# A four-layer attention kernel on one core: four hundred operations of the last quarter take other places in the order table

## The chip, the core and the metric

The kernel runs on one core of a Trainium2 chip. Its engines run beside each other, each in the order of its own instruction stream: TensorE (PE in the profile; PEld is its loading of weights), VectorE (DVE), ScalarE (ACT) and GpSimd (POOL). SyncE (SP) and ACT issue the transfers here. The metric is the device time of one execution in microseconds (us).

## The reference

Four residual layers in the order A, B, A, B act on x of 2048 rows and 512 columns, with 32 heads of 16:

```python
def _A_ref(x, wqkv, wo):                      # attention within a window of 256 rows
    ...
    scores = jnp.einsum("bhqd,bhkd->bhqk", q, k) * (Dh ** -0.5)
    mask = (idx[:, None] - idx[None, :] >= 0) & (idx[:, None] - idx[None, :] < W)
    scores = jnp.where(mask[None, None], scores, -1e9)
    p = _softmax(scores, axis=-1)
    o = jnp.einsum("bhqk,bhkd->bhqd", p, v)
    return (...)(o, 0, 2, 1, 3).reshape(B, S, D) @ wo
def _B_ref(x, wqkv, wo):                      # linear attention
    ...
    phi = lambda t: jnp.where(t > 0, t + 1, jnp.exp(t)) + 1e-6
    pq, pk = phi(q), phi(k)
    kv = jnp.einsum("bhsd,bhse->bhde", pk, v)
    num = jnp.einsum("bhqd,bhde->bhqe", pq, kv)
    den = jnp.einsum("bhqd,bhd->bhq", pq, z)[..., None] + 1e-6
    return (...)(num / den, 0, 2, 1, 3).reshape(B, S, D) @ wo
x = x + _A_ref(_layernorm(x), A_wqkv, A_wo)   # and so on: B, A, B
```

## The kernel before

The residual stays on chip as 16 tiles of 128 rows (`xres`), in four superblocks I of four tiles. The program is a list of 2583 operations, and each says which engines it may run on, what it depends on and which buffers it takes: one of 8 PSUM banks of `psb`, or a place in a small ring (`xn`, `oT`, `xnT`, `pks`, `vs`, `ln`). No scheduler decides the order when the kernel is built. The string `ORDER` (line 214 on) holds it, written out by hand or by a search: an entry such as `2537P1` says that operation 2537 comes next, on PE, with PSUM bank 1; A is ACT, V DVE, G POOL, S SP; `4F2` is four filler matmuls into bank 2 (L463). `Planner.run` walks the string and emits every operation on its engine. So the places in the string set the order of each engine, and an engine waits at an instruction whose input or buffer is not ready, with all that stands behind it. A bank that was given to one operation is free for the next only when its last reader is done.

The steps that the change and the prediction touch, with their lines:

- **Attention of the second A layer** (the last of it lies at 305 to 371 us of the trace): scores on PE (L823), two exps of 128x1024 on ACT (L834, L837), masks on DVE (L852, a multiply for one or two windows of 64) or POOL (L857, an affine select for each window), product with v on PE (L880), division on DVE (L893, L894). Projections are four matmuls in two halves (L537), and a copy out of PSUM is L527 on ACT or DVE.
- **Closing layernorm**: the attention's output projection is added to the residual (DVE L736, L738), then the squares on ACT (L612), the inverse root on ACT (L592, L593) or POOL (L595, L596), the normalized tile on ACT (L626), DVE or POOL (L628), and its transpose by PE (L566), copied out by ACT or DVE (L569).
- **phi of layer B**: exp on ACT (L948), min and add on DVE or POOL (L951), add and max on DVE (L954); v's copy is L981; kv is summed by PE (L995) and DVE (L1002).
- **End stage**: kv times wo (L1063, woB to `wkv`). For each pair of superblocks PE makes the denominators (L1078), ACT its logarithm and exp, which is the reciprocal (L1083, L1084), and a bf16 part of it (L1090), DVE the rest (L1093); PE spreads that to all rows (L1106) and DVE multiplies `pqT` by it, two columns at a time (L1110). Then each tile is projected by `wkv` (L537) and added to the residual: on DVE (L729, or in two halves L704 for tile 2), or, for tiles with i%3 = 1, by an ACT copy (L720) and a POOL add (L724). A put (L731, L707) to the output is issued by SP or ACT.

The tile order of the last projections is 1, 3, 2, 0, 7, then 4, 5, 6 (with the second pair's spreads between), then those of I=3 and at the end those of I=2. An ACT copy, a POOL add or a put is behind each.

Of the kernel before, what the change touches and what calls it, by code (L numbers as in the profile page):

```python
# [214 lines left out]
24S 2G 5G 4G 15H 14H 53V0 0G 11G 58V1 17H 54A 68A1 6G 16H 63V2 3G 59G 55V20 18H 19H 1G 10F0 56P5 60V0 64G 61P1 57A 62V  # L215
9G 69V 2F2 74P0 75A 7V 1F2 70P1 65V0 72P6 71A 66P3 20H 92P7 73A 21H 67V 93P 120P42 94A 80P0 122A 95S 76P6 81V 88P1 121A
77V 89P 23H 22H 78P2 350V0 90A 123G 124P64 82P0 126A 79V 351G 91S 84P1 125A 340V1 133P24 83A 127G 96P6 85V 134A 106P0
10G 97V 104P1 135A 107V 137P26 341G 105V 139A 86P0 138A 146P46 87V 27S 116P1 147A 335V2 98P0 117P 148A 99V 336G 150P42
136V 25S 112P0 345V3 151A 149G 113P 152A 159P64 118A 337V31 140G 102P2 114V 161A 35S 128P1 346G 129P 103V 130P 131P 160A
342V1 163P42 153G 132V 26H 165A 115S 347V2 162G 3F0 188P06 164A 634V1 100P2 189A 166G 141P5 154P4 101V 155P 142P 36H  # L220
143P 190A 635G 144P 28H 352V0 193P02 145V 156P 119S 12G 157P 194A 108P6 158V 167P7 168P 191G 169P 195A 109V 170P 199P04
171V 348P6 200A 353P3 196G 349V 338P7 172S0 354V 343P6 201A 339V 204P02 638V0 379P7 29S 205A 380P 202G 344V 636V32 192G
206A 381V 2F5 210P04 361P6 639G 637S 642V1 362P 211A 208G 110P7 363V 212A 31S 203G 224P02 30H 198G 640V0 225A 383P5 213G
111V 384P 197V 382S 226A 643G 229P06 385V 214P4 215P 230A 646V0 216P 32H 358P5 644V3 231A 647G 217P 228V 235P02 641S
218V 359P 209G 236A 207G 355P7 360V 219P6 645S 237A 933V2 240P04 356P 241A 648V1 220P 239G 357V 221P 649S 232G 222P 233G
242A 246P02 227V 387P7 234G 386S 247A 223V 388P 238G 245V 389V 248A 395P04 13G 664P6 396A 665P 249V 934G 390S 250P7 667V
251P 397A 244G 400P02 666V 252P 243G 401A 941V0 253P 399G 391P6 392P 254V 402A 176S1 405P04 393V 364P7 406A 403G 365P
255P6 407A 366V 394S 410P02 256P 398V 257P 411A 404V 409G 258P 678P7 259V 412A 679P 416P04 680V 260S3 417A 657P3 414G
408V 415G 658P 276V 418A 650P2 264S2 660V 432P06 651P 413V 434A 419G 420V 51S 367P5 421V 368P 433A 659V 422P4 423P 369V
424P 653A 33S 436G 437P06 425P 438A 652V 427P5 428P 426V 429P 439A 430P 442P02 431V 376P4 443A 440G 377P 942G 34H 370P5  # L230
444A 378V 447P06 371P 441V 935V20 448A 682P4 372V 683P 449A 435V 453P02 684V 675P5 454A 676P 446V 451G 685S 452V 450V
455A 2F4 469P60 677V 445V 471A 457V 2F4 474P24 458V 456V 49S 937V1 475A 464P1 459P0 465P 476A 460P 466P 41S 461P 470A
467P 462P 479P24 463V 173P7 472G 480A 39S 468V 174P 481A 175V 484P02 654P6 945V2 936S 655P 485A 482G 373P7 473V 477G
656V 374P 938G 486A 681S 490P04 375V 690P6 483G 491A 691P 946G 487V 492A 177P7 489V 939V0 178P 488G 478V 506P02 692A
494V 495G 493V 507A 693S 943V1 2F4 496P5 179V 501P4 508A 497P 511P06 498P 512A 510V 509G 502P 180V1 499P 47S 503P 513A
500V 504P 181G 516P02 686P5 517A 514V 505V 940S 184V3 518A 3F7 521P06 671P4 45S 48H 687P 522A 519V 947V2 672P 688V 523A
527P20 674V 948S 265P5 266P 529A 524V 526G 661P7 673V 944S 515G 662P 528A 267V 525G 261P6 520V 694P40 663A 689S 531V
532G 262P 695A 530V 533P7 263V 534P 696A 535P 272V0 699P42 538P6 700A 539P 698G 540P 182G01 536P 701A 541P 537V 704P04
# [1210 lines left out]
```

## Time and profile before

| | us |
|---|---|
| time, median of 3 runs | 416.8 |
| lowest and highest run | 416.27, 418.25 |
| span of the profiled execution | 414.3 |
| TensorE busy in it | 395.2 (95%) |
| ACT, DVE, POOL busy | 368.8 (89%), 355.0 (86%), 239.2 (58%) |

The span is the time from the first to the last instruction that the profiler recorded of one execution; about 2.5 us of the median lie outside it. In all but the last of the page's 40 slices the granted clock of TensorE is 9 tenths or more. The chain of waits that ended last is for 66% on PE, 15% on ACT and 12% on DVE. The rows on which the prediction rests are in the section after next.

### The profile page before, as it was taken

How to read it: one execution, taken by the hardware profiler on the slowest of the kernel's cores; microseconds unless marked ns; L12 is line 12 of the kernel's file. 1: busy time of each engine (PE TensorE's matmuls, PEld its weight loads, DVE VectorE, ACT ScalarE, POOL GpSimd, SP SyncE). 2: the span in 40 equal slices, each digit the busy share in tenths (PEclk: the TensorE clock that was granted, in tenths of full speed). 3: DMA queues.
4: the chain of work that ended last, by engine and by line, in shares of the span. 5: the costliest groups of instructions: out<-in, count | busy, mean ns of one | idle time of the engine just before them, and what ended most of it. 6: DMA issues, size and time to landing. Idle time of an engine off the chain costs nothing.

```text
span 414.3 us, 15373 instructions
## 1 busy us (share of the span) xinstructions
PE 395.2 (95%) x6277; PEld 219.3 (53%) x6347; DVE 355.0 (86%) x844; ACT 368.8 (89%) x496; POOL 239.2 (58%) x505
## 2 busy tenths in 40 slices
PE   7998999999999999999999999999999999999995
PEld 3565555555555555643565555555555555565342
DVE  5899898888769988689998999998789588889895
ACT  5999999999999999678999999999999999977731
POOL 7578524344576667923774688554427476585432
PEclk9999999999999999999999999999999999999998
DMA  8233226440313122100032212322111311300024
GB/s 245 83 95 100 64 76 110 110 77 24 89 25 80 35 55 26 28 4 0 22 72 41 55 45 64 71 38 53 41 49 34 54 30 40 54 14 14 3 69 138
DMA packets 65306, 24.11 MB, mean 58 GB/s; under 512 B 46160, under 2 KB 65232, under 8 KB 65232
## 3 DMA queue, kind: packets, MB, share of 16 engines
q1 hardware_dynamic: 63168, 21.65, 23.5%
q10 hardware_dynamic: 2064, 1.44, 1.1%
q8 instruction: 50, 0.82, 0.8%
q14 instruction: 24, 0.20, 0.2%
HBM read 6.29 MB, written 2.10 MB: 20 GB/s over the span
## 4 chain that ended last, share of the span: by engine, by line
PE 66%; ACT 15%; DVE 12%; issue 4%; POOL 2%; ACTq 0%; POOLq 0%; DVEq 0%
PE psb L537 41%; PE psb L880 14%; PE psb L823 8%; ACT pt L834 7%; ACT pt L837 7%; DVE pt L852 2%; DVE kall L788 1%; PE psb L995 1%; DVE qT L527 1%; PE psb L566 1%; DVE kall L773 1%; PE psb L463 1%; DVE vst L527 1%; PE psb L1106 1%; DVE ln L661 1%
## 5 line engine op out<-in xcount | busy, mean ns | idle before, releaser
L857 POOL TENSOR_SCALAR_AFFINE_SELECT pt<-pt 128x256 bf16<-128x256 bf16 x285 | 121.3, 453 | 110.2 <-ACT pt L837 66.7
L837 ACT ACTIVATE pt<-psb 128x1024 bf16<-128x1024 f32 (+2 forms) x156 | 156.2, 1017 | 4.4 <-PE psb L823 3.0
L834 ACT ACTIVATE pt<-psb 128x1024 bf16<-128x1024 f32 (+2 forms) x156 | 156.7, 1014 | 3.6 <-PE psb L823 2.3
L880 PEld LDWEIGHTS <-pt 128*128 128x128 bf16 x2880 | 81.4, 96 | 16.5 <-issue 5.0
L880 PE MATMUL psb<-vbd,pt 128*128 128x34 bf16 x2880 | 85.1, 178 | 2.4 <-ACT pt L834 1.0
L537 PE MATMUL psb<-xnT,wA 128*128 128x512 bf16 (+1 forms) x305 | 65.1, 335 | 2.2 <-DVE o_sb L894 0.3
L537 PE MATMUL psb<-wB,xnT 128*128 128x512 bf16 x237 | 62.4, 379 | 1.7 <-issue 0.5
L823 PE MATMUL psb<-qT,kall 32*128 32x256 bf16 (+4 forms) x1664 | 62.6, 242 | 0.6 <-ACT pt L834 0.4
L537 PEld LDWEIGHTS <-xnT 128*128 128x128 bf16 x384 | 33.4, 97 | 37.0 <-issue 5.3
L823 PEld LDWEIGHTS <-kall 32*128 32x128 bf16 x1664 | 28.0, 92 | 45.8 <-issue 42.2
L852 DVE TENSOR_TENSOR pt<-pt,tri 128x512 bf16<-128x512 bf16 (+1 forms) x133 | 49.5, 399 | 2.8 <-ACT pt L837 1.9
L537 PEld LDWEIGHTS <-wA 128*128 128x128 bf16 x320 | 27.4, 97 | 26.1 <-issue 7.7
L537 PE MATMUL psb<-woA,oT 128*128 128x512 bf16 x120 | 32.8, 380 | 1.2 <-issue 0.6
L537 PE MATMUL psb<-wA,xnT 128*128 128x512 bf16 x115 | 32.3, 380 | 1.5 <-ACT pt L837 0.5
L537 PE MATMUL psb<-xnT,wB 128*128 128x512 bf16 x119 | 32.1, 380 | 0.9 <-issue 0.5
L537 PE MATMUL psb<-wkv,pqT 128*128 128x512 bf16 (+1 forms) x126 | 30.2, 373 | 0.5 <-issue 0.2
L894 DVE TENSOR_TENSOR o_sb<-psb,rall 128x256 bf16<-128x256 f32 x64 | 27.2, 424 | 2.4 <-DVE rall L893 0.2
L893 DVE RECIPROCAL rall<-psb 128x16 f32<-128x16 f32 x64 | 16.1, 251 | 13.7 <-PE psb L880 9.4
L661 DVE BATCH_NORM_STATS2 ln<-xres 128x6 f32<-128x512 f32 (+1 forms) x39 | 26.6, 682 | 1.2 <-DMA xres<-in_A_x_dram 1.1
L596 POOL TENSOR_TENSOR ln<-ln,mhalf 128x1 f32<-128x1 f32 x38 | 22.0, 578 | 3.2
L948 ACT ACTIVATE pks<-psb 128x512 bf16<-128x512 f32 x32 | 19.5, 614 | 3.8 <-PE psb L537 3.4
L527 DVE CAST qT<-psb 128x512 bf16<-128x512 f32 (+1 forms) x32 | 19.2, 602 | 3.9 <-PE psb L537 3.7
(133 smaller groups left out, 523.6 us busy)
## 6 DMA issues: line engine op xcount, KB each, us to landing
vbd<-vst SPq DMA_DIRECT2D x128, 34.0 KB, 1.9
wB<-in_B_wqkv_dram SPq DMA_DIRECT2D x6, 256.0 KB, 3.5
out_dram<-ost SPq DMA_DIRECT2D x10, 128.0 KB, 1.8
xres<-in_A_x_dram SPq DMA_DIRECT2D x4, 256.0 KB, 3.2
xnT<-xn SPq DMA_TRANSPOSE x50, 2.4
out_dram<-ost ACTq DMA_DIRECT2D x5, 128.0 KB, 2.8
wA<-in_A_wqkv_dram SPq DMA_DIRECT2D x1, 512.0 KB, 7.5
xres<-in_A_x_dram SPq DMA_DIRECT2D x1, 512.0 KB, 8.7
```

What stands on the lines that cost most here:

```text
L527: (nc.scalar.copy if e == "ACT" else nc.vector.tensor_copy)(dst(), src())
L537: nc.tensor.matmul(t["t"][:], lhsT=lhs(c), rhs=rhs(c), start=(c == 0), stop=(c == NCT - 1))
L596: nc.gpsimd.tensor_tensor(out, out, mhalf[:, 0:1], op=ALU.pow)
L661: nc.vector.bn_stats(t["st"], x())
L823: nc.tensor.matmul(psb[:, sT.k + x if x < 2 else sS.k + x - 2, at * 64:(at + w) * 64], lhsT=kbd[half(m)][32 * x:32 * x + 32, tt, m % 4, :, :],
L834: nc.scalar.activation(body[:, 0:2, 0:w_all, :], psb[:, sT.k:sT.k + 2, 0:w_all * 64].rearrange("p x (s c) -> p x s c", c=64), ACT.Exp, sca ...
L837: nc.scalar.activation(body[:, 2:4, 0:w_all, :], psb[:, sS.k:sS.k + 2, 0:w_all * 64].rearrange("p x (s c) -> p x s c", c=64), ACT.Exp, sca ...
L852: nc.vector.tensor_tensor(v, v, mt, op=ALU.mult)
L857: nc.gpsimd.affine_select(out=v, in_=v, compare_op=ALU.is_ge, fill=0.0, base=1 if kind == 0 else -2, pattern=[[0, 4], [2 * sg, 64]], chann ...
L880: nc.tensor.matmul(t["O"][:, x, g, :, :], lhsT=parts[b][0][:, s0:s0 + 2, :], rhs=vbd[half(m)][:, m % 4, :, 4 * tt + g, :], start=(n == 0), ...
L894: nc.vector.tensor_tensor(o_sb[:, u0:u0 + nu, P * tt:P * tt + P].rearrange("p u (h e) -> p u h e", e=DH), Ov[:, :, :, 0:DH], r.to_broadcas ...
L948: nc.scalar.activation(dst(), ps()[:], ACT.Exp)
```

## The change

Only the string `ORDER` changes, and it grows by four lines, so that every line number below it is larger by 4 (L537 is L541 after). One of its lines at the end, before and after:

```diff
-2578S 2555A 2559P 2574A 2545P7 2560V0 2546P 2556G2 2569A 2549P0 2561S 2547V0 2550P 2557S 2548A 2551V3 2552S
+2568V0 2555A 2582A 2545P6 2569S 2556G1 2559P 2578S 2546P 2560V0 2549P2 2547V2 2557A 2550P 2561S 2536S 2551V1 2548S
```

The operations, their work, the fillers and the number of matmuls are the same. Up to 310 us of the trace of before every engine's own order is the same; from there on orders and buffers differ. Fifty operations change engine: 19 from POOL to DVE and 15 from DVE to POOL (mostly masks, and some of L951, the layernorm's apply and L628), four copies from DVE to ACT (three of v, L981, and one of L569), one inverse root each way between POOL and ACT and one apply from ACT to DVE (tiles 14 and 15), and nine puts between SP and ACT (five to ACT, four to SP). In 147 places another bank or ring place is taken.

In the attention, PE now has six halves of projections of layer B (`bq` of I=1 and 2) and tile 12's k ahead of the last products with v; before they stood behind them, from 370 to 379 us. ACT has three copies or exps for layer B ahead of the last exps of attention.

The first place shown is DVE at the closing layernorm of tiles 14 and 15 (their rows are L736, L740 after; `xn<-xres` is the normalized tile). Before:

```order
L569 COPY oT<-psb 128x512
L628 TENSOR_SCALAR xn<-xres,lnm,lrs 128x512
L951 TENSOR_SCALAR pks<-pks 128x512
L954 SCALAR_TENSOR_TENSOR pks<-psb,pks 128x512
L736 SCALAR_TENSOR_TENSOR xres,lsum<-psb,xres 128x512
L738 TENSOR_SCALAR lnm<-lsum 128x1
L736 SCALAR_TENSOR_TENSOR xres,lsum<-psb,xres 128x512
L738 TENSOR_SCALAR lnm<-lsum 128x1
L951 TENSOR_SCALAR pqT<-pqT 128x512
L954 SCALAR_TENSOR_TENSOR pqT<-psb,pqT 128x512
L1002 TENSOR_TENSOR kvs<-psb,kvs 128x132
```

After:

```order
L923 SCALAR_TENSOR_TENSOR okt,okw<-rall_154 128x128 x2
L955 TENSOR_SCALAR pqT<-pqT 128x512
L985 CAST vs_162<-psb 128x16x32
L958 SCALAR_TENSOR_TENSOR pks<-psb,pks 128x512
L931 TENSOR_REDUCE okb<-okw 128x1
L740 SCALAR_TENSOR_TENSOR xres,lsum<-psb,xres 128x512
L742 TENSOR_SCALAR lnm<-lsum 128x1
L740 SCALAR_TENSOR_TENSOR xres,lsum<-psb,xres 128x512
L742 TENSOR_SCALAR lnm<-lsum 128x1
L632 TENSOR_SCALAR xn<-xres,lnm,lrs 128x512
L1006 TENSOR_TENSOR kvs<-psb,kvs 128x132
L573 COPY xnT<-psb 128x4x128
```

The checks (L919, L927 before), a phi and a copy of v now stand ahead of the residual sums, and the apply of tile 14 (L632 after) stands on DVE right behind them; before it was POOL's. On PE two halves fewer stand between tile 14's output projection and its transpose.

The second place is the end stage on ACT: the reciprocal of the second pair of superblocks (the only L1083, L1084 and L1090 in these rows). Before:

```order
L720 COPY o_sb<-psb 128x512
L1083 ACTIVATE psb<-psb,eps 128x512
L1084 ACTIVATE psb<-psb 128x512
L1090 CAST pks<-psb 128x512
L731 DMA out_dram<-ost 128x512
```

After:

```order
L952 ACTIVATE pqT<-psb 128x512
L1087 ACTIVATE psb<-psb,eps 128x512
L1088 ACTIVATE psb<-psb 128x512
L724 COPY o_sb<-psb 128x512
L1094 CAST pks<-psb 128x512
L735 DMA out_dram<-ost 128x512
```

The copy of tile 1 (L720, L724 after) moved from ahead of the reciprocal to between its exp and its bf16 part. On PE, the denominators that this reciprocal reads (L1078) stand two projection items later: behind the second half of tile 3 and one half of tile 2.

The third place is DVE in the same stage; each L1110 (L1114 after) is the multiply of two columns of one superblock, in the order I=0, then 1, then 3, then 2. Before:

```order
L951 TENSOR_SCALAR pqT<-pqT 128x512
L1110 TENSOR_TENSOR pqT<-pqT,psb 128x2x512 x2
L954 SCALAR_TENSOR_TENSOR pqT<-psb,pqT 128x512 x2
L1110 TENSOR_TENSOR pqT<-pqT,psb 128x2x512 x2
L729 TENSOR_TENSOR ost<-psb,xres 128x512
L704 TENSOR_TENSOR ost<-psb,xres 128x256
L1093 SCALAR_TENSOR_TENSOR pks<-pks,rest,psb 128x512
L729 TENSOR_TENSOR ost<-psb,xres 128x512
L704 TENSOR_TENSOR ost<-psb,xres 128x256
L1110 TENSOR_TENSOR pqT<-pqT,psb 128x2x512 x4
L729 TENSOR_TENSOR ost<-psb,xres 128x512 x8
```

After:

```order
L1114 TENSOR_TENSOR pqT<-pqT,psb 128x2x512 x2
L955 TENSOR_SCALAR pqT<-pqT 128x512
L958 SCALAR_TENSOR_TENSOR pqT<-psb,pqT 128x512 x2
L1114 TENSOR_TENSOR pqT<-pqT,psb 128x2x512 x2
L708 TENSOR_TENSOR ost<-psb,xres 128x256
L733 TENSOR_TENSOR ost<-psb,xres 128x512
L708 TENSOR_TENSOR ost<-psb,xres 128x256
L1097 SCALAR_TENSOR_TENSOR pks<-pks,rest,psb 128x512
L733 TENSOR_TENSOR ost<-psb,xres 128x512
L1114 TENSOR_TENSOR pqT<-pqT,psb 128x2x512 x2
L733 TENSOR_TENSOR ost<-psb,xres 128x512 x2
L1114 TENSOR_TENSOR pqT<-pqT,psb 128x2x512 x2
```

Three residual sums instead of two stand ahead of the second L1093, two more (tiles 5 and 6) stand between the pairs of the last four multiplies, and one L951 moved behind the first two multiplies. On SP the put of tile 7, which was the first of the last part of that queue, is now the third from its end.

## Rows read from the trace of the kernel before

**Rows 1.** Busy us by engine (x instructions), PE clock, DMA share, GB/s, five stretches.

```profile
305.00:350.20 45.20, 43.89 (x855) 24.99 (x861) 36.48 (x85) 44.31 (x52) 29.74 (x71) 1.00 0.22 43
350.20:385.00 34.80, 34.13 (x517) 19.26 (x521) 30.85 (x81) 27.88 (x44) 20.34 (x27) 1.00 0.13 25
385.00:393.60 8.60, 7.98 (x75) 2.95 (x76) 7.84 (x18) 6.64 (x12) 4.01 (x7) 1.00 0.01 3
393.60:409.60 16.00, 15.81 (x82) 6.66 (x84) 14.96 (x21) 4.76 (x8) 6.34 (x5) 1.00 0.30 102
409.60:414.30 4.70, 0.00 (x0) 0.00 (x0) 0.66 (x1) 0.00 (x0) 0.00 (x0) 0.77 0.33 110
```

**Rows 2.** Timeline of PE in attention: start, us, operation [idle before <-releaser].

```profile
316.08 1.02 PE L537 MATMUL psb<-xnT,wA 128*128 128x512 bf16 x3 [0.18 <-DVE o_sb L894]
...
333.92 0.38 PE L537 MATMUL psb<-wB,xnT 128*128 128x512 bf16 x1 [0.32 <-ACT pt L834]
```

**Rows 3.** Operations by form, 305 to 410 us: busy us, mean ns of one.

```profile
L857 POOL TENSOR_SCALAR_AFFINE_SELECT pt<-pt 128x256 bf16<-128x256 bf16 x57 | 24.3, 454 | 19.6 <-ACT pt L837 15.2 <-ACT pt L834 4.3
L951 POOL TENSOR_SCALAR pqT<-pqT 128x512 bf16<-128x512 bf16 x5 | 9.6, 1924 | 8.8 <-ACT pqT L948 8.6
L852 DVE TENSOR_TENSOR pt<-pt,tri 128x256 bf16<-128x256 bf16 x13 | 3.9, 309 | 0.2 <-ACT pt L837 0.2
L951 DVE TENSOR_SCALAR pqT<-pqT 128x512 bf16<-128x512 bf16 x11 | 3.6, 333 | 0.6 <-ACT pqT L948 0.4
L628 DVE TENSOR_SCALAR xn<-xres,lnm,lrs 128x512 bf16<-128x512 f32 x1 | 0.8, 751 | 0.0
```

**Rows 4.** Timeline, closing layernorm of tile 14: DVE, POOL and PE.

```profile
374.88 0.69 DVE L736 SCALAR_TENSOR_TENSOR xres<-psb,xres 128x512 f32<-128x512 f32 x1
...
377.45 0.77 POOL L628 TENSOR_SCALAR xn<-xres,lnm,lrs 128x512 bf16<-128x512 f32 x1
...
378.94 0.39 PE L566 MATMUL psb<-identb,xn 128*128 128x128 bf16 x4
```

**Rows 5.** Timeline of the junction to the end stage: PE and DVE.

```profile
390.00 0.39 PE L1063 MATMUL psb<-woB,pks 128*128 128x512 bf16 x1 [0.30 <-DVE pks L569]
...
385.80 0.15 DVE L927 TENSOR_REDUCE okb<-okw 128x1 bf16<-128x8 f32 x1
...
389.86 0.73 DVE L1093 SCALAR_TENSOR_TENSOR pks<-pks,rest,psb 128x512 bf16<-128x512 bf16 x1
```

**Rows 6.** Timeline of PE in the end stage.

```profile
395.00 0.61 PE L1078 MATMUL psb<-pqT,zc 128*32 128x512 bf16 x8
395.55 3.64 PE L537 MATMUL psb<-wkv,pqT 128*128 128x512 bf16 x19
399.12 0.60 PE L1106 MATMUL psb<-pks,spread 32*128 32x512 bf16 x4
...
401.59 7.94 PE L537 MATMUL psb<-wkv,pqT 128*128 128x512 bf16 x35
```

**Rows 7.** Timeline of ACT in the end stage.

```profile
394.68 0.59 ACT L720 COPY o_sb<-psb 128x512 f32<-128x512 f32 x1 [1.51 <-PE psb L537]
395.67 0.66 ACT L1083 ACTIVATE psb<-psb,eps 128x512 f32<-128x512 f32 x1 [0.41 <-PE psb L1078]
...
396.97 0.59 ACT L1090 CAST pks<-psb 128x512 bf16<-128x512 f32 x1
```

**Rows 8.** Timeline of DVE in the end stage.

```profile
397.87 0.74 DVE L1093 SCALAR_TENSOR_TENSOR pks<-pks,rest,psb 128x512 bf16<-128x512 bf16 x1
...
399.55 4.62 DVE L1110 TENSOR_TENSOR pqT<-pqT,psb 128x1024 bf16<-128x1024 bf16 x4
...
409.57 0.69 DVE L729 TENSOR_TENSOR ost<-psb,xres 128x512 bf16<-128x512 f32 x1 [0.17 <-PE psb L537]
```

**Rows 9.** Puts issued after 405 us: KB each, median us from issue to landing.

```profile
out_dram<-ost SPq DMA_DIRECT2D x7, 128.0 KB, 2.6
out_dram<-ost ACTq DMA_DIRECT2D x3, 128.0 KB, 3.9
```

More of the change, by code (lines that the diff above doesn't have):

```diff
@@ new lines @@
+501P4 508A 497P 511P06 498P 512A 510V 502P 509G 180V1 499P 503P 47S 513A 504P 500V 181G 940S 516P02 48H 517A 686P5
+514V 505V 45S 518A 184V3 3F7 521P06 46H 671P4 522A 519V 687P 947V2 672P 948S 688V 523A 527P20 674V 265P5 529A 526G
+266P 524V 944S 515G 673V 661P7 528A 525G 662P 267V 261P6 689S 520V 663A 532G 694P40 531V 262P 530V 695A 533P7 263V
+534P 696A 535P 272V0 699P42 538P6 700A 539P 698G 540P 182G01 536P 701A 541P 537V 704P04 273G 542V 705A 543S1 952P3
+953P 268V2 703G 706A 709P06 547S0 668P2 954V 710A 669P 274V3 970P3 670V 555S2 711A 715P04 708V 971P 702V 716A 697V
@@ new lines @@
+1618A 1462P 1873G 1611S 1590P7 1463V 1619A 1591P 2178V32 1622P40 1464P6 1623A 1592V 1465P 2179G 1466P 1467P 1624A
+1874S 1880G 1627P24 1468V 2175P7 1629A 2176P 1626G 1881V 1593P6 2177V 1628A 1594P 1615G 1882S 1633P04 1625V 1595V
+2169P7 1634A 1632G 2170P 1620G 1631V 1473S1 1616V 1630G 2172P6 1635A 2171V 1649P02 2173P 1621V 1469S2 1650A 1637V
+1636G 1584P4 2174V 1638G 1585P 1651A 1639P7 1586V 1640P 1641P 2182A0 1652G 1654P20 1644P6 2186V1 1655A 2183G 1645P
+1642P 1877V 1646P 1656A 1643V 1647P 1653G 1878S 2187G 1659P24 1648V 1660A 1911P1 1389V0 1657G 1912P 2180G 1661A
@@ new lines @@
+1754V 1768S2 1908P5 1938A 1936V 1909P 2222P4 1939A 1910V 1772S3 1942P06 1395V1 2223P 1943A 1941G 1792V 2209P5 1764S0
+2210P 2224V 1944A 1935G 1948P20 2211V 1901P4 1950A 1760S1 1902P 1947G 1945G 1769P5 1903V 1949A 1964P60 1396S 1478G
+1940V 1486P44 1946V 1965A 1951V 1487P 1952V 1953G 1770P 1966A 1959P6 1771V 1954P7 1960P 1488A 1969P20 1955P 1489V
+1971A 1961P 1490V 1956P 1962P 1970A 1957P 1974P04 1958V 1975A 1972G 1765P3 1963V 1967G 1766P 1976A 1973V 1979P06
+1479V1 2215P2 1767V 1480S 1980A 2216P 1978G 1761P5 2217V 1981A 1762P 1985P02 1763V 2218P4 1986A 1983G 1784V1 2219P
@@ new lines @@
+1984G 1499P52 1977G 1987A 2220V 1968G 2001P06 1500P 1982V 2221S 2002A 1988V 1494P21 1990V 1989V 1495P 2003A 1501V
+1991P4 1992P 1993P 1496A 2006P06 1497V 1996P5 2007A 1997P 1498V 2225S 1994P 1998P 2008A 1995V 1999P 2011P02 2000V
+1773P4 2012A 2010G 1776V0 1774P 2226P5 1484S 2013A 1775V 2016P06 1777G 2227P 2017A 2015V 1507P30 2228V 1508P 2018A
+2009V 2229S 2022P04 1509V 2023A 2021V 2019G 2F2 1515P74 1780V2 1516P 2024A 2014G 2038P20 2020V 2005G 1517V 1502P63
+2039A 1503P 2004V 2027G 2025V 2026G 1530P7 1788V3 2040A 1531P 1778G30 2033P3 2034P 1504A 2041V 2043P40 1532A 1789G
@@ new lines @@
+1796V 1519V 1802P 2242V 2083S0 1797V 2250P04 1803A 2249G 2080P7 2252A 1804V 1809P60 1805V 2087S2 1810P 2251A 2081P
+2107V 2256P42 2082V 1811A 2255G 2076P1 2258A 2238G 2077P 1812V 2244G 1813V 1798P00 2248G 2257A 1799P 2078V 2270P62
+1800V 1806P12 2272A 2259G 2095V2 1807P 1814P04 2237G 2271A 1808V 2275P42 2254G 1815P 2091V3 2276A 2260P1 2261P 1816V
+2262P 2092G 2277A 2263P 2281P46 2264V 2088P0 2282A 2280G 2253V 2089P 2273G 2265P1 2283A 2090V 2279G 2286P24 2266P
+2103V1 2230P0 2287A 2278G 2267P 2268P 2104G 2288A 2292P62 2269V 2231P 2285G 2293A 2274V 1822P41 2232V 1823P 2290V
@@ new lines @@
+2349P 2350P 2360A 2351P 2121P70 2352V 2122P 1527A 2342G 1524V 2363P40 2307P2 2364A 1528V 2116P61 1529V 2308P 2365A
+2117P 2309V 2353P5 2118A 2354P 2123V 2157P4 2314A21 2369P20 2362V 2119V 2311P7 2315G 2370A 2120V 2355P 2158P 2361G
+2371A 2356P 2312P 2357V 2124P62 2159A 2373G 2313V 2374P20 2316G 2129P52 2376A 2160V 2130P 2372G 2317S 2368V 2318V1
+2125P 2131A 1827P0 2161V 2375A 2319G 1828P 2366V 1837P7 1829A 2320G 2379V 2380P42 1838P 1830V 2381A 2378G 2321S
+2132P13 2133P 2382A 2367G 2142P5 2143P 2377G 2134A 2383V 2415P44 2144A 2135V 2384P2 1831V 2126A 2389P3 2390P 2136V
```

230 lines of the change are left out of this document (102 added, 128 removed).

## The prediction

> **What bounds the kernel now.** I read the page first: PE is busy for 95% of the span, and two thirds of the chain of waits is PE. Since the orders of all engines agree up to about 310 us, I then cut the rest by stage [rows 1] and asked in each which engine leaves no gaps. From 305 to 350.2 it is ACT: 44.31 of 45.20 us busy with the exps of attention, while PE idles 45.20 - 43.89 = 1.31 us. From 350.2 to 385 it is PE, with 0.67 us of gaps in 34.80. From 385 to 393.6 DVE is busy 7.84 of 8.60: kv, the last phi, the first reciprocal's rest and the first multiplies follow each other there. From 393.6 to 409.6 PE is busy 15.81 of 16.00, and then come 4.70 us with one residual sum and the last puts. So there is little to win: the gaps of PE after 305 us are 1.31 + 0.67 + 0.62 + 0.19 = 2.79 us, and part of these are records that the trace lacks. A change that only reorders has those gaps and the tail to take from, and can lose by opening new ones.
>
> **The sum's own time.** The profiled execution spans 414.3 us and the median of the runs is 416.8, so 2.5 us lie outside. The change touches only what is inside, and I add what I find to 416.8. A measurement of this kernel can tell about 0.5%, or 2.1 us, from no change.
>
> **Part 1, attention to 350 us.** ACT binds, and it gets the same exps and copies up to that point in a slightly different order, so the sum of its work is the same: 0. What can go are the waits of PE that are real ones, 0.18 us for a division and 0.32 us for an exp [rows 2], if the new banks and the swapped exps (L837 ahead of L834) fit better. PE is not the bound there, so at most ACT's own idle time goes: 45.20 - 44.31 = 0.89 us, of which some is between instructions; I bound the gain by the two waits, 0.50, and the loss by one wait of the same size more, 0.4. I take a gain of 0.2, less than half of the two.
>
> Masks change between DVE and POOL here in both directions. One on POOL takes 0.454 us per window, one on DVE 0.309 [rows 3]; the 0.15 us lies behind the exps, with other products of v in front, and I cost it at nothing. If that cover is gone, it is one of the rivals.
>
> **Part 2, 350 to 385 us.** PE binds and has the same matmuls. Six halves and tile 12's k go ahead of the last products with v, which therefore come some 1.3 us later on PE; three ACT items of about 0.6 us each, 1.8 together, go ahead of the last exps. The scores that these exps read come 1.3 us later too, so ACT has that time for the extra items, and the exps end just in front of the products: 0, at worst 0.4.
>
> The place where a wait is new is the closing layernorm of tile 14. Before, its residual sum starts at 374.88 and PE's transpose at 378.94, and POOL's apply ends at 377.45 + 0.77 = 378.22, so 0.72 us were spare [rows 4]. Now four halves of projections have left the stretch of PE between the output projection and the transpose, and two others came in. A half is two matmuls; one takes (7.94 - 0.39) / 34 = 0.22 us in a row [rows 4, 6], so PE is there 4 x 0.22 = 0.88 us sooner: 0.72 - 0.88 = -0.16. The inverse root on ACT instead of POOL and the apply on DVE (0.751 [rows 3] against 0.77) take about the same time. But five DVE items that stood behind the residual sums now stand in front (two checks, a min and add of 0.333 [rows 3], a copy of v, one phi); each found its place where DVE had been waiting for PE, so I count not their sum, but 0.05 of lateness beyond the -0.16. PE waits 0.2 there; between 0 (PE's new halves come in just as late) and 0.6 (the root waits on ACT behind one exp of 0.6).
>
> **Part 3, the junction.** DVE binds from kv's last sum to the first L1093 at 389.86 [rows 5]. In that stretch it has the same phis as before, but the reduction of the checks, 0.15 us, has gone ahead [rows 5]; the copy of the transposed kv (L569) stands one phi sooner, so PE's wait of 0.30 us for it goes [rows 5], but PE then waits for L1093 instead, which keeps its place behind the same phis. The min and add that moved behind the first two multiplies was not in the way: the spread on PE ended just when it ended. Gain 0.15, and about as much for a bank that is taken closer to its last reader: 0, from -0.3 (the wait in full) to +0.3 (the same again).
>
> **Part 4, the end stage.** The reciprocal of the second pair is a chain of PE (L1078), ACT (three instructions) and DVE (L1093), then the spread (L1106) on PE. Before, L1078 ended at 395.00 + 0.61 = 395.61, ACT started at 395.67 and finished at 396.97 + 0.59 = 397.56 [rows 7], and L1093 at 397.87 + 0.74 = 398.61 [rows 8]; PE reached the spread at 399.12 [rows 6]: 0.51 us spare, less a hand-over. Now L1078 comes two items later, two matmuls of 512 columns and four of 256: 4 x 0.22 = 0.88 us. ACT's copy of 0.59 us [rows 7] is inside the chain. Together +1.47, of which the 397.87 - 397.56 = 0.31 that L1093 waited for its own queue is absorbed: it now ends at 398.61 + 1.47 - 0.31 = 399.77. PE's part in front of the spread grows by one item net, 0.44: it arrives at 399.56 and waits 0.21, with a hand-over 0.25.
>
> Then DVE: one residual sum of 0.69 [rows 8] in front of the multiplies, which before stood there as well; the first pair of multiplies takes 4.62 / 2 = 2.31 us [rows 8] and ends at 399.77 + 0.69 + 2.31 = 402.77. PE has the same projections in front of I=3's first tile as before, where it came to it after tile 6, at 401.59 + 0.88 = 402.47 [rows 6]; late by the 0.25 it is there at 402.72. Two more sums of 0.69, then the last pair: 402.77 + 1.38 + 2.31 = 406.46; PE arrives at I=2's first tile after four tiles of 0.88, at 402.77 + 3.52 = 406.29. So PE waits 0.25 + 0.05 + 0.17 = 0.47, which I round down for a sum of DVE that overlaps the next by some hundredths in every row of such sums. Part 4 costs 0.4; it costs 0 if the two items in front of L1078 run in gaps, and 1.2 if the two near misses both miss by the 0.4 by which such a place can be late.
>
> **Part 5, the tail.** The last sum still ends 0.69 us after PE's last matmul, and the last put is still SP's [rows 8]. Tile 7's put comes into the last bunch, one put more; nine puts change between SP and ACT. In this stretch a put took 2.6 us to land from SP and 3.9 from ACT [rows 9]. The transfers of the last 4.70 us moved 110 GB/s with the DMA engines busy 0.33 of the time [rows 1], so 333 GB/s while busy, or 0.39 us for the 131 KB of one put. One put more in front of the last one costs 0.4 us at most, and one fewer, since others now leave earlier, gains as much: I take 0.
>
> **Sum:** -0.2 + 0.2 + 0 + 0.4 + 0 = +0.4 us, so 416.8 + 0.4 = 417.2.
>
> **Rivals.** First, *the waits go*: PE's two waits (0.50), the 0.30 at the junction and 0.4 of the tail go, and parts 2 and 4 find their cover: -1.2, or 415.6. With the whole 1.31 of the first stage instead of 0.50 it is -2.01, or 414.8, just about what can be told. For it speaks that the moves in attention put projections where PE waited; against it that ACT binds there and has no less to do. Chance 0.14.
>
> Second, *the end stage turns to DVE*, slower: if L1093 ends later than the 399.77 of part 4, each further tenth goes straight through, since L1106, four multiplies and two sums stand behind it in one row (0.69 + 2.31 + 1.38 + 2.31 = 6.69 us) and PE has tiles for only as long. Its price: the 0.59 of the copy, if it waits for tile 1's matmuls as ACT did for 1.51 us before the change [rows 7], plus the two sums of 1.38, so 1.97, beside the 0.4 of the tail: with half of it 417.8 (forecast 0.4 not counted twice), with all of it and the tail 416.8 + 1.97 + 0.4 = 419.2. For it speaks that both arrivals in part 4 are within 0.2 us. Chance 0.16.
>
> Third, *masks come late*, slower: POOL takes 1.924 us for a min and add that DVE does in 0.333 [rows 3], and two of these go to POOL; a mask behind one waits up to 1.9 us, and the product with v with it. It decides where PE has less than that in front, and costs up to 1.9: 418.7. Against it: POOL is busy 29.74 of 45.20 us [rows 1], and two others go the other way. Chance 0.08. The Trainium skill's page "GPSIMD Engine Reference", at its beginning, calls GpSimd wrong for ordinary elementwise work, where VectorE is "roughly 2× faster". For the masks the rows show less, 0.454 against 0.309, and for the min and add more, 5.8 times. By the rule the 15 moves to POOL, at 0.45 against half of that, could cost 15 x 0.23 = 3.4 us if none were covered, by the rows for masks 15 x 0.145 = 2.2; the 19 moves the other way give more than that back by either, so that as a whole the exchange would not be a loss, and the sum takes neither.
>
> Fourth, *nothing shows*: every new wait is covered and no old one goes, 416.8. Chance 0.20; the forecast itself has 0.42.
>
> **How the numbers follow.** The parts' low ends are -0.5, 0, -0.3, 0 and -0.4, -1.2 in all, and with part 1's whole gaps -2.01; the high ends 0.4, 0.4 + 0.6, 0.3, 1.2 and 0.4, 3.3 in all, which won't come together. I take 415.2 to 419.3: it leaves out the best of the first rival and the upper end of the sum. Faster by over 0.5% (under 414.7) needs the whole of the first rival and a little of the scatter between runs, half its 0.14: 0.07. Slower by over 0.5% needs over 418.9: about half of the second and third rivals and a little of the forecast's upper end, 0.15. The rest, 0.78, is within 0.5%.
>
> **What would show it.** In the profile of the changed kernel L1093 of the second pair (L1097) ends about 1.1 us later, PE has one new wait of some 0.3 us before the second L1106 (L1110) and one of some 0.2 us before tile 14's transpose, and PE ends at about 410. ACT's last exp before 350 us ends within 0.3 us of before. It is wrong if gaps of PE over 1 us in all open in attention, if the last pair of multiplies ends later than 407, or if the part up to 310 us differs by more than a few tenths.

## The result: slower by 0.84%, outside the range

The changed kernel takes 420.62 us (median of 6 runs, 420.09 to 421.49) against 417.22 for the kernel before, taken beside it (6 runs): the ratio is 1.0084, with a 95% interval from 1.0063 to 1.0104. I had forecast 417.2 us and no change that can be told, in a range up to 419.3. The time lies 1.3 us above it; 0.4 of that is the kernel before itself, which I had taken at 416.8 from three runs.

The span of the profiled execution is 418.4 us, 4.1 more than before. Of that, 0.65 us is there already at 302 us, where all orders are still the same (the same group of products starts at 302.87 against 302.21); among the kernels of the experiments that share the changed kernel's whole order up to there, it starts between 302.33 (e4) and 303.56 (e11). I take it as no part of the change; without it 3.5 us remain, and the runs show 3.4.

The page of after looks like that of before: PE is busy for 95%. So I cut both traces at the same operations. Each row is a stretch from the start of one operation to the start of the next: a product with v of superblock 2, one of the last scores of superblock 3, a kv sum, the first denominators, the first spread, the first tile of the end stage, PE's end, the end. The columns are those of [rows 1]. Before:

```profile
312.80:349.73 36.93, 35.73 (x757) 21.19 (x760) 28.86 (x64) 36.36 (x43) 25.44 (x61) 1.00 0.23 42
349.73:382.94 33.21, 32.70 (x500) 18.66 (x501) 29.62 (x79) 26.86 (x43) 19.86 (x28) 1.00 0.14 26
382.94:387.24 4.30, 4.14 (x80) 1.97 (x81) 3.14 (x9) 2.11 (x4) 1.86 (x6) 1.00 0.02 6
387.24:390.78 3.54, 3.08 (x24) 1.19 (x25) 3.44 (x9) 3.35 (x7) 0.82 (x2) 1.00 0.01 2
390.78:393.62 2.84, 2.67 (x14) 0.79 (x14) 2.81 (x6) 2.37 (x5) 1.92 (x1) 1.00 0.00 0
393.62:409.53 15.91, 15.80 (x82) 6.65 (x83) 14.91 (x20) 4.76 (x8) 6.34 (x5) 1.00 0.30 101
409.53:414.30 4.77, 0.00 (x1) 0.00 (x0) 0.69 (x1) 0.00 (x0) 0.00 (x0) 0.78 0.34 114
```

After:

```profile
313.45:351.15 37.70, 36.00 (x756) 20.98 (x760) 31.35 (x75) 36.35 (x44) 20.73 (x51) 1.00 0.20 41
351.15:384.12 32.97, 32.45 (x500) 18.30 (x501) 26.86 (x71) 27.03 (x44) 21.45 (x34) 1.00 0.12 27
384.12:388.71 4.59, 4.21 (x81) 1.96 (x82) 3.93 (x9) 2.86 (x5) 1.66 (x6) 1.00 0.01 4
388.71:392.68 3.97, 2.99 (x22) 1.18 (x23) 3.03 (x7) 3.50 (x6) 0.86 (x2) 1.00 0.00 0
392.68:396.05 3.37, 2.95 (x16) 0.79 (x15) 3.13 (x6) 2.17 (x4) 1.92 (x1) 1.00 0.00 0
396.05:412.31 16.26, 16.14 (x84) 6.79 (x84) 14.91 (x20) 4.48 (x8) 6.30 (x5) 1.00 0.26 90
412.31:418.40 6.09, 0.00 (x0) 0.00 (x0) 0.78 (x2) 0.00 (x0) 0.00 (x0) 0.87 0.34 113
```

The lengths, after less before: attention +0.77, the next stretch -0.24, kv +0.29, the first reciprocal +0.43, the first spreads and multiplies +0.53, the end stage +0.35, the tail +1.32; 3.45 us in all. PE's clock was granted in full up to its end in both. The loss has no single place, and its two largest parts, the junction (0.29 + 0.43 + 0.53 = 1.25) and the tail, are the ones that I had priced at nothing.

What PE waits for shows the first half of it. The view of waits of PE, us in total, times, longest, for 312 to 413 us of after:

```profile
PE psb L467 <- DVE pks L1097: 0.8, 1, 0.8
PE psb L541 <- DMA oT<-o_sb: 0.6, 1, 0.6
PE psb L541 <- issue: 0.5, 3, 0.2
PE psb L467 <- ACT pqT L952: 0.4, 1, 0.4
PE psb L827 <- ACT pt L841: 0.2, 1, 0.2
PE psb L999 <- DVE pks L958: 0.2, 1, 0.2
PE psb L884 <- ACT pt L841: 0.2, 1, 0.2
```

The two L467 are fillers, matmuls whose result nobody is meant to read. Their rows in the timeline of PE, with the wait in front:

```profile
392.15 0.38 PE L467 MATMUL psb<-identb 128*128 128x512 bf16 x1 [0.84 <-DVE pks L1097]
...
395.42 0.38 PE L467 MATMUL psb<-identb 128*128 128x512 bf16 x1 [0.42 <-ACT pqT L952]
```

A filler writes a PSUM bank too. The string puts them into banks 2 and 4; in before these were free, and in after bank 2 holds the first reciprocal until L1097 has read it, and bank 4 a projection of layer B's q that phi's exp reads. PE stops at the filler, and the projection, the check and the spread behind the first one come late.

The second filler does more harm than its wait. The string has `2468A 1F4 ... 2470V`: 2468 is the exp, and 2470, phi's max (L958), reads bank 4 once more. It runs behind the filler:

```profile
396.12 1.29 DVE L958 SCALAR_TENSOR_TENSOR pqT<-psb,pqT 128x512 bf16<-128x512 f32 x2
```

So one block of phi in the changed kernel (128 columns of superblock I=3) is made from the filler's numbers. `Planner.run` asks of every operation whether its bank is free, but not of a filler. The same holds in e1, e4, e6, e8 and e11, which keep this filler as it is, and not where bank 7 is used (e3, e13, e16).

The tail is read from SP's timeline. Before, and then after, the puts that SP issues last:

```profile
408.99 1.07 SPq L731 DMA_DIRECT2D out_dram<-ost  x1
...
410.29 0.33 SPq L731 DMA_DIRECT2D out_dram<-ost  x1
```

```profile
412.26 1.80 SPq L735 DMA_DIRECT2D out_dram<-ost  x1
...
414.93 0.52 SPq L735 DMA_DIRECT2D out_dram<-ost  x1
```

Most of the last eight puts are issued in 0.33 to 0.52 us, but one of them took 1.07 us before and 1.80 after. In both traces a 16 KB packet of instructions runs at that time in the queue q8 of the page (50 such packets in either span, one for about 253 of the 12,666 instructions that PE and its weight loads execute, so I take them for PE's), from 408.43 to 409.69 and from 412.08 to 413.67. Before, one put stood behind the long one, and its sum had just ended (409.57 + 0.69 = 410.26 [rows 8]; issued at 410.29). After, two stood behind it, tile 8's and the last. The last sum:

```profile
412.40 0.69 DVE L733 TENSOR_TENSOR ost<-psb,xres 128x512 bf16<-128x512 f32 x1
```

It ended at 413.09, and its put was issued at 414.93, 1.84 us later. The put then landed in 2.1 us, where the last put of before took 2.6, so that 1.3 us of the delay are left in the tail.

### The profile page after: what moved, and what is told of

The parts are those of the page before. It is cut to its first block, busy times and chain, and to the rows that moved or that the text cites. A ratio compares the mean times of both kernels' runs of the same rounds, so it can differ in the third digit from the quotient of the medians.

```text
span 418.4 us, 15369 instructions
## 1 busy us (share of the span) xinstructions
PE 397.2 (95%) x6276; PEld 219.8 (53%) x6347; DVE 355.3 (85%) x845; ACT 369.5 (88%) x498; POOL 236.4 (56%) x501
## 4 chain that ended last, share of the span: by engine, by line
PE 64%; ACT 17%; DVE 10%; issue 4%; POOL 2%; DMA 2%; SPq 0%; ACTq 0%; POOLq 0%; DVEq 0%
PE psb L541 39%; PE psb L884 13%; ACT pt L841 8%; ACT pt L838 8%; PE psb L827 7%; DVE pt L856 1%; PE psb L467 1%; DMA oT<-o_sb 1%; PE psb L999 1%; PE psb L570 1%; DVE qT L531 1%; DVE ln L665 1%; PE psb L1110 1%; DMA vbd<-vst 1%; DVE kall L792 1%
## 5 line engine op out<-in xcount | busy, mean ns | idle before, releaser
L541 PE MATMUL psb<-xnT,wA 128*128 128x512 bf16 (+1 forms) x305 | 65.6, 338 | 1.6 <-issue 0.3
L541 PE MATMUL psb<-wB,xnT 128*128 128x512 bf16 x234 | 62.5, 379 | 1.6 <-issue 0.6
L856 DVE TENSOR_TENSOR pt<-pt,tri 128x512 bf16<-128x512 bf16 (+1 forms) x135 | 50.7, 402 | 3.7 <-ACT pt L841 2.7
L541 PEld LDWEIGHTS <-xnT 128*128 128x128 bf16 x384 | 33.3, 97 | 36.6 <-issue 4.6
L541 PEld LDWEIGHTS <-wA 128*128 128x128 bf16 x320 | 27.6, 98 | 25.9 <-issue 7.3
L541 PE MATMUL psb<-woA,oT 128*128 128x512 bf16 x120 | 33.4, 380 | 1.7 <-DMA oT<-o_sb 0.6
L541 PE MATMUL psb<-wA,xnT 128*128 128x512 bf16 x115 | 32.3, 380 | 1.7 <-ACT pt L841 0.5
L541 PE MATMUL psb<-xnT,wB 128*128 128x512 bf16 x121 | 32.6, 380 | 0.5 <-issue 0.2
L541 PE MATMUL psb<-wkv,pqT 128*128 128x512 bf16 (+1 forms) x126 | 30.2, 373 | 0.4 <-issue 0.2
L958 DVE SCALAR_TENSOR_TENSOR pks<-psb,pks 128x512 bf16<-128x512 f32 x32 | 22.0, 686 | 0.5
```

The lines of the kernel that those rows point to most:

```text
L541: nc.tensor.matmul(t["t"][:], lhsT=lhs(c), rhs=rhs(c), start=(c == 0), stop=(c == NCT - 1))
L856: nc.vector.tensor_tensor(v, v, mt, op=ALU.mult)
L958: nc.vector.scalar_tensor_tensor(out=dst(), in0=ps()[:], scalar=1.0 + 1e-6, in1=dst(), op0=ALU.add, op1=ALU.max)
```

## The experiments

Times are given by their ratio to the kernel before, run beside them on the same chip (the 95% interval is about 0.0015 to each side where no other is given); 0.001 is 0.42 us. The string is broken into other lines in some of them, so line numbers can be 7 smaller than in after.

### e1 and e2: which half

Both orders agree with a cut at one projection of q (385 us): what stands ahead of it in one kernel is what stands ahead of it in the other, but for a few operations, and no buffer has to change. e1 is before's string up to the cut and after's from it, e2 the reverse.

> The order of before up to the last projections of layer B's q (385 us), and from there on the order, engines and banks of after. The two traces put the loss of 3.4 us at three places: 0.5 in attention, 1.3 at the junction, 0.3 in the end stage and 1.3 behind the last matmul. Theory 1 (the loss lies behind 385 us): +2.9 us against before, 420.1. Rival (the attention's order costs most, by what it leaves late for later stages): under +1.2, 418.4 or less.

Measured: 1.0068, +2.8 us.

> The mirror of the run before: the order of after up to 385 us, and before's from there on. Theory 1: +0.5 us against before, 417.7. Rival: +2.2 or more.

Measured: 1.0037, +1.5 us. Most of the loss lies behind 385 us, as theory 1 says, but e2 misses its 0.5, and the two halves add to 4.3 us where the whole costs 3.4. The early part costs more than its stages in after: this cut brings a longer wait at kv of its own (5.06 us for the stretch that takes 4.30 and 4.59), and PE's wait for a transfer in attention is 0.9 us instead of 0.6.

### e3, e5 and e10: the fillers

e3 in the changed kernel:

```diff
-2482A 1F2 2477P6 ... 2468A 1F4 2517P6
+2482A 1F7 2477P6 ... 2468A 1F7 2517P6
```

> The changed kernel with its two last filler matmuls in PSUM bank 7, which nobody uses then, instead of banks 2 and 4, which the first reciprocal and a phi still read. Theory 2 (the fillers wait for those banks, 0.84 and 0.42 us, and hold the spread and the projections behind them): 0.6 to 0.9 us faster than the changed kernel, and no wait at a filler in the trace. Rival (the chain over VectorE sets the junction, and PE would wait for it one instruction later): 0.0 to 0.2 us.

Measured: 1.0061 against 1.0084, about 1.0 us faster. The two stretches in its trace:

```profile
388.88:392.32 3.44, 2.90 (x21) 1.27 (x22) 3.08 (x8) 3.23 (x6) 0.86 (x2) 1.00 0.00 0
392.32:395.22 2.90, 2.90 (x14) 0.80 (x13) 2.76 (x6) 2.35 (x5) 1.55 (x1) 1.00 0.00 0
```

3.44 and 2.90 us instead of 3.97 and 3.37, so 1.0 us, and before had 3.54 and 2.84. No filler waits. PE now waits 0.41 us for VectorE ahead of the spread, as the rival said, but what was late at the filler came earlier, and the gain is at the upper end. Both stretches together take 6.34 us, against 7.34 in after and 6.38 in before: at the junction, the banks of two matmuls that compute nothing cost the whole difference. In this trace the end stage gives 0.15 us of it back.

The mirror in the kernel before. First both fillers into the banks that hold the reciprocal and the phi there:

> The kernel before with nothing changed but the bank of its two last filler matmuls: banks 6 and 1, which hold the first reciprocal and a phi there, as banks 2 and 4 do in the changed kernel. Theory 2 (the wait of a filler holds all of PE behind it): +0.8 to +1.2 us, 417.8 to 418.2, and two waits at fillers in the trace. Rival (banks matter only together with the new order): 0.0 to +0.3 us.

Measured: 1.0002. It tells little about the wait: here both fillers stand ahead of the last readers in the string, as the second one of after does, so they didn't wait for these and wrote over what was still to be read. The next one puts the reader ahead of the filler, and no engine's order changes:

```diff
-2468A 1F2 2477P3 2491V 2486P2
+2468A 2491V 1F6 2477P3 2486P2
```

> Instead of e5, whose fillers overwrote what was still to be read: the kernel before with one change, the first of the two last fillers put into bank 6, which the first reciprocal holds, and behind its last reader, so that it waits for it (L1093), as in the changed kernel. Theory 2: PE waits 0.3 to 0.6 us at that filler, the spread comes as much later, and the time grows by 0.3 to 0.6 us. Rival (another wait just behind it, for the first multiplies, takes it in): 0.0 to 0.1 us.

Measured: 1.0015 (1.0002 to 1.0027), +0.6 us. Its row:

```profile
391.94 0.38 PE L460 MATMUL psb<-identb 128*128 128x512 bf16 x1 [1.16 <-DVE pks L1090]
```

The wait is longer than forecast, since this filler stands further forward on PE; it takes in the 0.30 us for L569 behind it [rows 5], and the junction grows by 0.84 us. One filler in a bank that is still held is enough to slow the old order too, though the lower end of the interval is close to no change.

### e4, e9, e14 and e15: the tail

e4 in the changed kernel:

```diff
-2531S 2580P ... 2561S 2536S 2551V1 2548S
+2531S 2536S 2580P ... 2561S 2551V1 2548A
```

> The changed kernel with two puts elsewhere: tile 8's issued by ACT instead of SP, tile 7's ahead of four others on SP, as both stood before. In the trace of after SP takes 1.80 us to issue one put (412.26 to 414.06), while PE's last fetch of instructions goes through the transfer engines, and the last put stands two behind it: issued at 414.93 though its tile was ready at 413.10. Theory 3 (a put that is issued in that fetch holds its queue): 0.9 to 1.3 us faster than the changed kernel. Rival (the transfers themselves are held by the fetch, whoever issues them): 0.0 to 0.3 us.

Measured: 1.0077 against 1.0084: 0.3 us, with overlapping intervals, and the trace shows 5.72 us from PE's end to the end, 0.37 less. Here the rival is nearer. ACT's two last puts in this trace:

```profile
411.64 2.26 ACTq L728 DMA_DIRECT2D out_dram<-ost  x2
```

The first was issued in 0.36 us and the second in 1.61 (412.30 to 413.91): ACT is held as SP is, and the last put, begun at 412.99 on SP, took until 413.90: both queues go on at the same moment, 0.4 us after the packet of instructions ends (411.96 to 413.51).

e9 is e1 with the cut at the first tile of the end stage, so that the junction is before's.

> The order of before up to the first tile of the end stage (394.4 us), and after's from there: the later denominators, the copy inside the reciprocal, the sums among the multiplies, and the puts. Theory (the losses add up by place: end stage 0.35 as the prediction's part 4, behind the last matmul 0.9 to 1.3): +1.2 to +1.7 us against before. Rival (the end stage's order costs only together with a late junction): +0.4 or less.

Measured: 1.0025, +1.05 us. In its trace the end stage and the tail take 16.10 and 5.65 us:

```profile
393.65:409.75 16.10, 15.99 (x82) 6.65 (x83) 14.82 (x20) 4.66 (x8) 6.31 (x5) 1.00 0.27 91
```

So 0.2 us are the order of the end stage and 0.9 the tail. e14 then changed the two puts alone in the kernel before; tile 7's late put keeps its ring place, so another had to be found for tile 13:

```diff
-2536S ... 2573G2 ... 2561S 2547V0 2550P 2557S 2548A
+2573G3 ... 2561S 2536S 2547V0 2550P 2557S 2548S
```

> The kernel before with the puts of tiles 7 and 8 alone changed as in the changed kernel: tile 8's on SP instead of ACT, tile 7's third from SP's end (with another place in the ring for tile 13, so that it needn't wait for it). Theory 7 (SP's queue behind the put that the fetch holds): the last put is issued 0.4 to 1.0 us after its tile is ready, and the time grows by 0.4 to 1.0 us. Rival (when the fetch comes, which the matmuls' order sets, decides): 0.0 to 0.2 us.

Measured: 1.0033, +1.4 us, more than either theory. The reason is a side effect:

```profile
412.49 0.69 DVE L726 TENSOR_TENSOR ost<-psb,xres 128x512 bf16<-128x512 f32 x1 [2.14 <-DMA out_dram<-ost]
```

The last sum takes the ring place that I had given to tile 13, and waits until that tile's put has landed. e15 gives it tile 15's place (2551V1 instead of 2551V3):

> As e14, but tile 9's sum takes the ring place of tile 15, whose put has landed long before. Theory 7 (SP's queue behind the put that the fetch holds): the last put is issued 0.3 to 0.8 us after its sum's end, and the time grows by 0.2 to 0.7 us. Rival (the puts' queues don't matter while the fetch comes 1.1 us before PE's end): 0.0 to 0.1 us.

Measured: 1.0023 (1.0003 to 1.0042), +0.95 us, above theory 7's 0.7. The end stage is as before, the tail is 1.1 us longer:

```profile
393.73:409.65 15.92, 15.81 (x82) 6.65 (x83) 14.90 (x20) 4.75 (x8) 6.34 (x5) 1.00 0.27 93
409.65:415.50 5.85, 0.00 (x0) 0.00 (x0) 0.69 (x1) 0.00 (x0) 0.00 (x0) 0.77 0.35 115
```

The last put waits for three long issues of 1.12, 0.65 and, its own, 1.01 us. Only the first began within the packet in q8 (408.86 to 409.82); the other two began as 8 KB packets ran in q14, which the page also calls instruction (410.30 to 410.63, 411.52 to 412.37). So the two puts are enough in the old order (e15), and taking them back is not enough in the new one (e4). The fetch also comes at other moments:

| kernel | last fetch against PE's end, us | order of the end / the two puts | PE's end to the end, us |
|---|---|---|---|
| before | -1.10 | before / before | 4.77 |
| e12 | -0.97 | before / before | 4.78 |
| e7 | -0.62 | before / before | 5.31 |
| e15 | -0.79 | before / after | 5.85 |
| e4 | -0.22 | after / before | 5.72 |
| e9 | -0.13 | after / after | 5.65 |
| after | -0.23 | after / after | 6.09 |

The traces of the other kernels scatter: with the order and the puts of before the tail takes 4.7 to 5.3 us (e2, e5, e10 and e13 too), with both of after 5.6 to 6.3 (e1, e3, e6, e8 and e11 too), and with one of the two 5.7 to 6.0 (e16 too). So the order of the end or the two puts alone makes the tail about 1 us longer, and no more is seen with both. That the later fetch is what the new order brings to it fits the table, but no run moved the fetch alone as far, so it isn't shown.

### e6, e7, e11 and e12: can the fetch be moved

> The changed kernel with 20 matmuls of 16 columns more at 7 us, where PE waits 0.8 us for the layernorm. They make PE's program 40 instructions longer, counted before the end. Theory 4 (PE's last fetch comes at a fixed count of PE's instructions, every 256, and happens to fall on the last puts): the fetch now comes some 20 matmuls or 4 us before PE's last matmul instead of 0.2 us, and the last put lands 0.9 to 1.4 us sooner after it: 419.2 to 419.7. Rival (the fetch belongs to the end of PE's program): it stays 0.2 us before the end, and the time is the same or 0.4 longer.

Measured: 1.0089 (1.0074 to 1.0104); the fetch came 0.23 us after PE's end.

> The same 20 matmuls in the kernel before, whose last fetch comes 1.1 us before PE's last matmul. Theory 4: the fetch comes 5 us before it, the last put is no longer held, and the time is 0.3 to 0.8 us shorter than before: 416.2 to 416.7. Rival: 0.0 to +0.4.

Measured: 0.9991 (0.998 to 1.0002); the fetch came 0.62 us before PE's end. Theory 4 falls: the regular fetches shifted (the one before the last from 387.64 in after to 405.31 in e6), the last one stayed with the end. The edit in both was a loop of 20 such matmuls in the filler's function, run by `120F0` in the string:

```diff
+nc.tensor.matmul(psb[:, k, 0:16], lhsT=identb[:], rhs=identb[:, 0:16], start=True, stop=True)
```

Then the hint for the jump over the code that isn't run (`AHEAD`, P: 9 to 30):

> The shift of e6 did not move the last fetch: it stayed 0.2 us from PE's end. Theory 6: it is asked for by PE's branch hint for the jump over the safe network, which stands 9 operations before PE's end (AHEAD in the planner). Here the hint stands 30 operations ahead, in the changed kernel: the fetch comes some 8 us sooner, before most of the puts, none of the last four puts takes over 0.6 us to issue, and the time falls by 0.8 to 1.4 us. Rival (the fetch comes at the end itself, whatever the hint): no shift and 0.0.

Measured: 1.0078 (1.0057 to 1.0098); fetch 0.22 us before PE's end, SP's long issue 1.74 us.

> The same hint in the kernel before, whose last fetch comes 1.1 us before PE's end. Theory 6: the tail shrinks by 0.3 to 0.8 us, and this version is the fastest. Rival: 0.0.

Measured: 0.9998 (0.9986 to 1.001). Theory 6 falls too. With the end of before the fetch came 0.6 to 1.1 us ahead of PE's end, with the end of after between 0.23 ahead and 0.23 behind, in all kernels. What sets the moment stays open.

### e8, e13 and e16: attention, and whether the parts add up

e8 in the changed kernel, tile 9's half later on PE:

```diff
-2249G 2080P7 2252A 1804V 1809P60 1805V 2087S2 1810P 2251A 2081P
+2249G 2252A 1804V 1809P60 1805V 2087S2 1810P 2251A 2080P7 2081P
```

> The changed kernel with one half of tile 9's output projection (operation 2080) behind two halves of a k projection instead of ahead of them, nearly as before. In the trace of after it waits 0.59 us there for the transfer that transposes o. Theory 5 (that wait is most of what attention lost): 0.3 to 0.6 us faster than the changed kernel. Rival (ScalarE sets attention, and what PE wins is waited for at the next exp): 0.0 to 0.2 us.

Measured: 1.0070 (1.0050 to 1.0089) against 1.0084, 0.6 us, in intervals that overlap; the trace shows 0.43 less in the first stretch:

```profile
313.54:350.81 37.27, 36.03 (x755) 21.13 (x761) 31.43 (x75) 36.25 (x44) 20.78 (x51) 1.00 0.20 42
```

That is 37.27 us against 37.70, of a loss of 0.77 there. The wait is this row of after:

```profile
330.97 0.39 PE L541 MATMUL psb<-woA,oT 128*128 128x512 bf16 x1 [0.59 <-DMA oT<-o_sb]
```

> The changed kernel with tile 9's half projection behind the two halves (as e8), the two fillers in bank 7 (as e3), and before's order, engines and banks from the first tile of the end stage on (the reverse of e9). If the places add up (0.45 + 1.0 + 1.2 of 3.4 us), +0.4 to +0.9 us remain against before: the rest of attention and 0.3 us at kv's last sum, where VectorE comes later. Rival (the losses hide others that come out when they go): +1.5 or more remain.

Measured: 1.0084 (1.0070 to 1.0098): nothing gained. The fillers' and tile 9's gains are in its trace, but the end stage, which has before's order, takes 17.7 us instead of 15.9:

```profile
398.87 3.19 PE L534 MATMUL psb<-wkv,pqT 128*128 128x256 bf16 x17 [1.30 <-DVE pqT L1107]
```

PE takes tile 7 early, as before did, and needs the multiplies of I=1 for it; VectorE comes from the order of after, in which a min and add moved behind the first multiplies and those of I=1 come later (here they end at 398.81). In the changed kernel tile 7 stands later on PE too: two moves that belong together.

> The changed kernel with tile 9's half projection later (e8), the two fillers in bank 7 (e3) and the two puts as before (e4). If the three add up as they were measured against the changed kernel (0.6, 1.0 and 0.8 us), it is 2.2 to 2.6 us faster than that, so +0.9 to +1.3 us against before. Rival (what one wins another wait takes): +2.0 or more remain.

Measured: 1.0049 (1.0031 to 1.0066), 1.45 us faster than after, not 2.2 to 2.6. In the trace attention gives its 0.43 and the junction its 1.0; the end stage takes 0.17 back and the tail gives 0.14, since the last put is held again: 0.93 us on SP from 411.76, in the packet of 410.74 to 412.30. What is left (2.05 us) is, by the trace, the tail with some 1.2, the end stage with 0.5, kv 0.29 and the rest of attention, 0.34, for which no run tells the cause. No version was faster than the kernel before by more than can be told.

## Why the prediction was wrong, part by part

**Part 1** (attention: -0.2, bounds -0.5 to +0.4; measured +0.77). The two waits of [rows 2] did go, as I had hoped: neither row is in after. Three others came: 0.59 us for a transfer, 0.24 and 0.19 for exps. I looked at ACT, DVE and POOL as those that PE could wait for, and not at the transposes that SP issues, though tile 9's half had been moved in front of two other halves, towards one of them. e8 shows that it was 0.43 of the 0.77. That ACT's work stays the same was right (36.36 and 36.35 us of that stretch), but its idle time grew from 0.57 to 1.35 us: the bound of one wait of 0.4 was too small, since a late PE makes the scores for the next exps late too.

**Part 2** (0 + 0.2; measured -0.24 for that stretch and +0.29 for the kv behind it). The late products with v cost nothing, as said. The wait at tile 14's transpose that I had priced at 0.2 is not there:

```profile
379.69 0.59 PE L541 MATMUL psb<-wB,xnT 128*128 128x512 bf16 x2
380.12 0.39 PE L570 MATMUL psb<-identb,xn 128*128 128x128 bf16 x4
```

What came instead is a wait of 0.22 us of kv for a phi on VectorE (the L999 of the view of waits), an operation that I had not costed. As a sum the part was within 0.2.

**Part 3** (the junction: 0, bounds -0.3 to +0.3; measured 0.43 + 0.53 = +0.96 without kv). This step failed. I followed the order of the operations and took the fillers for the same, because their number and place on PE are; 147 buffers had changed, and I asked of each operation's bank when it comes free, but not of the filler's, which has no operation. Their two waits, 0.84 and 0.42 us, are the whole of it: without them the junction takes 6.34 us (e3), and before 6.38. The first rival's 0.30 us for L569 [rows 5] did go, and was lost in the longer wait.

**Part 4** (+0.4; measured +0.35). Right in size; the chain up to the spread came as worked out, the rest by luck:

```profile
401.28 0.75 DVE L1097 SCALAR_TENSOR_TENSOR pks<-pks,rest,psb 128x512 bf16<-128x512 bf16 x1 [0.35 <-ACT pks L1094]
401.95 0.68 DVE L733 TENSOR_TENSOR ost<-psb,xres 128x512 bf16<-128x512 f32 x1
402.55 2.34 DVE L1114 TENSOR_TENSOR pqT<-pqT,psb 128x1024 bf16<-128x1024 bf16 x2
```

L1097 ends at 402.03, 5.98 us after the end stage begins, against 4.99 before (398.61 - 393.62): 0.99 later, where I had 1.16. PE starts the spread at 402.08, about 0.1 late instead of the 0.25. The waits at the first tiles of I=3 and I=2 that made up the rest of my sum are not there. The largest one is a step earlier, in the second spread, whose last matmul starts 0.19 us after the one before it; in before these two start together, at 401.28:

```profile
404.92 0.37 PE L1110 MATMUL psb<-pks,spread 32*128 32x512 bf16 x1
404.28 0.59 ACT L724 COPY o_sb<-psb 128x512 f32<-128x512 f32 x1
```

By the string it writes bank 6 (`2541P5` takes 5 and 6), which a projection holds (`2519P6`) until this copy, 2521, has read it, at 404.87. The same 0.19 us stand in e9, and they are its end stage's whole loss. So here too it was a bank, and I had not asked when it comes free.

**Part 5** (the tail: 0, bounds -0.4 to +0.4; measured +1.32). This step failed with the largest sum. I looked at the right place, one put more in front of the last, but priced the wrong thing: a transfer's 0.39 us, set against one put fewer, while the wait is in the issue, 1.80 us for one put, with the puts behind it on the same queue. That the two puts do it in the old order is shown (e15: +0.95), and in the new one they are not all (e4: 0.3 us won). It could be seen: before's SP took 1.07 us for the put at 408.99, and I had taken only the landing times [rows 9].

The **rivals** that I had named did not decide. The end stage did not turn to VectorE beyond part 4, no mask made PE wait for long, and the waits that went were outweighed. The bounds of parts 3 and 5 were made from waits of the same size as those in the trace, so that even all high ends together came to 3.3 us. One full filler wait (the 2.01 us between the denominators' end and L1093 in before) and one long issue (1.07) as bounds would have put the high ends 2.4 us higher. Of the signs that I had set, the last pair of multiplies ends at 408.34, past 407, but only because everything ahead of it is late: it is 12.3 us behind the start of the end stage, where I had 12.8.

## What to carry to other kernels

When an order table changes, ask of every instruction that writes a buffer when that buffer comes free, fillers and other work without a result too: a filler in a bank that is still read stops the engine that it was to keep busy, and one that stands ahead of the last reader overwrites what is to be read. Read the issue times of the last transfers one by one and put nothing behind the one that can be long: of the 1.84 us by which the last put came late here, 1.3 were left in the time. And a move of one engine's order is half of a pair: taking one back alone can cost more than the pair.

## What the runs showed of the hardware

While a packet of the queue q8 ran, which I take for PE's instructions, issuing a put could take 1.0 to 1.8 us instead of 0.33, on SP and on ACT alike (1.07 before, 1.80 after, 1.61 on ACT in e4, 1.19 in e9). In the trace of before, 9 of the 12 plain transfers that SP or ACT began to issue within such a packet took over 0.6 us; of the 139 that met no packet of instructions at all, none took over 0.61. In all 18 traces, 182 of 3,042 took over 0.7 us: 171 met a packet of q8, 8 one of q14 alone, and 3 neither. Why the one holds the other is not shown. The packet itself is 16 KB and took 1.26 us before and 1.59 after. The view of the DMA queues shows it for 412 to 413.8 us of after:

```profile
q8 instruction: 1, 0.02, 5.5%
```

Every span here ends with such a fetch close to PE's last matmul; neither 40 more instructions nor an earlier hint moved it away from there, and which of the last operations sets its moment was not found.
